# Selection state in PSUM, separate regions and locks, a loop of its own for the end, and earlier constants and loads, in a Fourier layer with routed experts

## The chip, the cores and the metric

The kernel runs on one core of a Trainium2 chip. Its engines are TensorE (PE; PEld is its weight load), VectorE (DVE), ScalarE (ACT), GpSimd (POOL) and SyncE (SP); transfers are issued on the queues of SP, ACT and POOL and carried by 16 DMA engines. The metric is the device time of one execution in microseconds, as the median of several runs; less is better.

## The reference

For each of 8 images x (3136 positions, 256 channels, float32) a Fourier layer is followed by a layer that sends 128 positions through a two-layer expert:

```python
X = rfft(x, axis=1)                              # 1569 frequencies
Yr = shrink(Xr @ w_r - Xi @ w_i + b_r, 0.01)     # shrink: sign(v) * max(|v| - 0.01, 0)
Yi = shrink(Xr @ w_i + Xi @ w_r + b_i, 0.01)
y = irfft(Yr + 1j * Yi)
scores = y @ w_gate                              # one per position
top = the 128 positions with the largest scores
out = y;  out[top] = y[top] + sigmoid(scores[top]) * (relu(y[top] @ w1) @ w2)
```

with w_r, w_i 256x256, w1 256x1024, w2 1024x256.

## The kernel before, in words

The transform of 3136 = 98 x 32 points is done in two stages of matmuls each way. Loads of x (`ld_x`) bring parts of an image, `fold` (on POOL in the steady state, 1.29 us for each of two instructions, line 392) adds and subtracts its halves, `s1` (line 403) does the first stage on PE and writes to a scratch array As in DRAM. The middle runs over 100 units, one per step t: `s2` (line 433) the second stage, read back from As; `spectral` (lines 226 to 228 and 466) the products with the weights, where ACT copies one part to SBUF (line 460), POOL adds the bias (line 462) and DVE adds both (line 466); `shrink` (lines 471, 473); and `s2i` (line 490) the first inverse stage, whose two PSUM tiles `pca` and `pcb` ACT copies to be stored to a scratch array Cs in DRAM (line 513) and DVE multiplies with the gate for the scores (line 501). `ld_c` loads Cs, `s1i` (line 550) does the last stage, and its results go to the output. An image has 8 pieces of `s1`, 12 or 13 units, and 8 pieces of `s1i`.

PE's banks of PSUM are full: pca and pcb are one bank each of 512 float32 per partition. Columns 0 to 255 hold the outputs of `s2i`. The second half of pcb holds a product of `spectral`; the second half of pca is shared by the routing: 64 columns for the counts of the selection (`sel_ps`), the rest for everything else (`route_ps`).

Routing is a set of Python generators, called threads, that are advanced once or twice per step by `turn` in phases "pe", "da", "db". A thread first computes scores (`score`, lines 518 to 527), then `select` finds the 128th largest score of each of its images by bits: per round DVE makes candidate words f from the threshold word w (line 243), compares all scores with them (line 247), sums (line 251); PE adds the counts over partitions (line 254); DVE turns the count into the next w (lines 266 to 269). A round takes one step: 17 rounds at 2 bits, 12 at 3 bits. Then `place` works out the indices (lines 276 to 327), four to five steps per image. The threads are images (0, 1) and (2, 3) at 2 bits, (4, 5), (6) and (7) at 3 bits. One lock, `lock`, is held by a thread while it scores or places an image, as both use route_ps. The experts are two more threads that `tick` advances once per step: `fetch` gathers the rows of an image, whose output must be complete, with an indirect transfer on POOL's queue; `ffn` (lines 340 to 374) takes ten turns per image, three of them idle, and uses one bank named "m".

The order of instructions on every engine and queue is that of the program. In step t the loop issues on SP the stores of the step before, loads of x for 21 steps later, loads of As 3 to 4 steps ahead, loads of Cs 2 steps ahead of use; then `s2` of the next unit, a piece of `s1` or `s1i`, the routing's phases, `spectral` with the phase "db" inside, the folds, the experts, `s2i` of the unit before, `shrink`. The loop runs on for 20 steps after the last unit with what is left: three pieces of image 6, all of image 7, whose Cs is loaded in steps 101 and 103, and routing. Constants of the routing are loaded and made in step 8 (`consts_b`, lines 211 to 217), and zeros for the padding rows of Cs in steps 8, 10 and 12 (`pads`, line 531, on POOL).

Of the kernel before, what the change touches and what calls it, by code (L numbers as in the profile page):

```python
# [10 lines left out]
F32 = mybir.dt.float32  # L11
# [89 lines left out]
def fourier_moe(ctx: ExitStack, tc: tile.TileContext, x, w_r, w_i, b_r, b_i, wg, w1, w2,  # L101
# [63 lines left out]

    sel_ps, route_ps = pca[:, D:D + 64], pca[:, D + 64:]

# [42 lines left out]
    def consts_b():  # L210
        ld(wq, t_wq)
        make_identity(nc, ident)
        ld(digits, t_dig)
        nc.gpsimd.dma_start(out=tm, in_=t_m)
        nc.gpsimd.iota(iota, [[1, 128 * NCHK]], base=0, channel_multiplier=0, allow_small_or_imprecise_dtypes=True)
        nc.gpsimd.iota(nrow, [[1, 1]], base=0, channel_multiplier=N2, allow_small_or_imprecise_dtypes=True)
        nc.gpsimd.iota(tcol, [[128, NCHK]], base=0, channel_multiplier=1, allow_small_or_imprecise_dtypes=True)

    def consts_moe(k):
# [10 lines left out]
    def select(bs, bits, thrs, at):  # L230
# [3 lines left out]
        while cuts[-1] > 0:  # L234
            cuts.append(max(cuts[-1] - bits, 0))
        w = None
        for hi, i in zip([32] + cuts, cuts):
            m = 2 ** (hi - i) - 1
            f = pool.tile([N1, nb, m], U32, name=f"f{nb}{m}", bufs=1)
            if w is None:  # L240
                nc.vector.memset(f, 0)
            else:
                nc.vector.tensor_tensor(out=f, in0=digits[:, 8 * i:8 * i + m].rearrange("p (o m) -> p o m", o=1).broadcast_to([N1, nb, m]),  # L243
                                        in1=w.broadcast_to([N1, nb, m]), op=ALU.bitwise_xor)
# [11 lines left out]
            tot = tot.rearrange("p (b m) -> p b m", b=nb)  # L256
            w2 = pool.tile([N1, nb, 1], U32, name=f"w{nb}")
            if w is None:
                nc.vector.tensor_scalar(out=w2.bitcast(I32), in0=tot, scalar1=cap - 0.5, scalar2=1.0, op0=ALU.is_ge, op1=ALU.subtract)
            else:  # L260
                d = pool.tile([N1, nb, 1], U32, name=f"d{nb}", bufs=1)
                if m == 1:
                    nc.vector.tensor_scalar(out=d, in0=tot, scalar1=cap - 0.5, scalar2=None, op0=ALU.is_ge)
                else:
                    ok = pool.tile([N1, nb, m], F32, name=f"ok{nb}{m}", bufs=1)
                    nc.vector.tensor_scalar(out=ok, in0=tot, scalar1=cap - 0.5, scalar2=None, op0=ALU.is_ge)  # L266
                    with nc.allow_low_precision(reason="whole numbers"):
                        nc.vector.tensor_reduce(out=d, in_=ok, axis=AX.X, op=ALU.add)
                nc.vector.scalar_tensor_tensor(out=w2, in0=d, scalar=i, in1=w, op0=ALU.logical_shift_left, op1=ALU.bitwise_xor)  # L269
            w = w2  # L270
        thr = pool.tile([N1, nb, 1], F32, name=f"thr{bs[0]}", bufs=1)
# [4 lines left out]
    def place(b, thr, slots):  # L276
# [4 lines left out]
        yield "pe"  # L281
        pt = route_ps[:2 * N2, :N1]
        nc.tensor.matmul(pt, mf, eye, start=True, stop=True)
# [3 lines left out]
        yield "pe"  # L287
        pp = route_ps[:N1, :2 * N2].rearrange("p (a c) -> p a c", a=2)
        nc.tensor.matmul(route_ps[:N1, :2 * N2], mt, upper[:2 * N2, :], start=True, stop=True)
        yield "da"  # L290
# [6 lines left out]
        yield "pe"  # L297
        pb = route_ps[:N1, :2]
        nc.tensor.matmul(pb, lower, cnt, start=True, stop=False)
# [5 lines left out]
        for k in range(NCHK):  # L305
# [8 lines left out]
            yield "pe"  # L314
            pi = route_ps[:n, :N2 + 2]
            for a in range(2):
# [12 lines left out]
    def gather(b, k, idx):  # L329
# [4 lines left out]
        return xe  # L334

    def prepare(b, k, idx, xe):
        n = min(128, cap - 128 * k)
# [13 lines left out]
    def hidden(b, k, xT, hs):  # L351
        n = min(128, cap - 128 * k)
        for q in range(FF // 512):
            ph = ps.tile([128, 4, n], F32, name="m", bufs=1)
            for f in range(4):
# [9 lines left out]
    def combine(b, k, idx, xe, ga, hs):  # L365
        n = min(128, cap - 128 * k)
        py = ps.tile([n, D], F32, name="m", bufs=1)
        for f in range(FF // 128):
# [147 lines left out]
    def score(b):  # L516
        p = route_ps[:NJ, :128]
# [5 lines left out]
        p = route_ps[:N1, :N2]  # L523
        for q in range(4):
            nc.tensor.matmul(p, wq[:, q, :], t[:, 64 * (q // 2) + q % 2:64 * (q // 2) + 64:2], start=(q == 0), stop=(q == 3))
        yield "da"
        nc.vector.tensor_copy(scores[:, b, :], p)

    def pads(k):
        z = pool.tile([128, 2, 2, 2 * D], F32, name="ot", bufs=2).rearrange("p r s x -> p (r s x)")  # L530
        nc.gpsimd.memset(z, 0.0)
        for q in range(2):
            ld(Csd[k][q, NH:].rearrange("m n d -> (m n d)").rearrange("(p x) -> p x", p=120), z[:120, :1024])

# [27 lines left out]
    def warm():  # L562
# [5 lines left out]
        for i in range(14):  # L568
            nc.tensor.matmul(p[:, i % 2], pr[:, :128], pr[:, :512], start=True, stop=True)

    YB, XB, KB, RB, AB = 2, 2, 1, 1, 3
    G, U = 13, 8
# [6 lines left out]

    lock = []  # L580

    def route(k, bs, bits):
        for b in bs:
            while done["s2i"] < b or lock:
                yield "pe"
            lock.append(k)
            yield from score(b)
            lock.clear()
            yield "da"
        yield from select(bs, bits, thrs, 32 * (k % 2))  # L590
        for b in bs:
            yield "db"
            while lock:
                yield "db"
            lock.append(k)
            yield from place(b, thrs[b], slots)
            lock.clear()

# [10 lines left out]
    def ffn():  # L609
        for e in range(B * NCHK):  # L610
            while not fetched:
                yield
            for _ in range(3):
                yield
            item = fetched[0]
            xT, ga = prepare(*item)
            yield
# [4 lines left out]

    threads = [[route(k, *a), "pe"] for k, a in enumerate((((0, 1), 2), ((2, 3), 2), ((4, 5), 3), ((6,), 3), ((7,), 3)))]
    ffns = [fetch(), ffn()]
# [30 lines left out]
    consts_a()  # L655
    consts_g(0)
    for i in range(U):
        fold(0, i, nc.gpsimd if i % 3 == 2 else nc.vector)
        s1(0, i)
        if i == 4:  # L660
            ld_x(1, 0)
            ld_x(1, 2)
        flush()
        issue_late()
# [8 lines left out]
    rest = [(b, i) for b in range(B) for i in range(U)]  # L673
    for t in range(-1, T + 20):
        flush()
# [4 lines left out]
        for u in (t + 3, t + 4):  # L680
            if 1 < u < T and (units[u][1] == G - 1) == (u == t + 3):
                ld_a(*units[u])
        for b, i in due(t - LAG + 2):
            if b < B - 1:
                ld_c(b, i)
        if t in (T + 1, T + 3):
            for i in range(4):
                ld_c(B - 1, i + 2 * (t - T - 1))
        if t % 2 == 0 and (t + 4) // 2 in range(2, 7):
# [45 lines left out]
        pair()  # L735
    flush()
    issue_late()
    while threads or ffns:
        turn("pe", "da", "db")
        tick(ffns)  # L740

# [26 lines left out]
```

## Time and profile before

| | us |
|---|---|
| median of 3 runs | 811.73 (802.27 to 816.13) |
| the profiled execution | 805.65 |
| its span, first to last instruction | 803.9 |

| engine | busy us | share of the span |
|---|---|---|
| PE | 657.2 | 82% |
| PEld | 490.1 | 61% |
| DVE | 515.5 | 64% |
| ACT | 361.6 | 45% |
| POOL | 299.7 | 37% |

The mean granted clock of TensorE is 0.919. The DMA engines moved 182.46 MB. Busy shares are means over the start, the 100 steps (to 717 us) and the end, which have different limits; the rows further down are therefore taken by stretch. In a row of a timeline, what stands in brackets is the engine's idle time before the instruction and what ended it. A wait that is put down to an instruction on DVE or ACT ended when that instruction did, in order of its queue.

### The profile page before, as it was taken

The numbers are of one execution on the slowest core, as the hardware profiler recorded it, in microseconds if no ns is written. First come the engines' busy times: TensorE is split into PE (matmuls) and PEld (weight loads), VectorE is DVE, ScalarE is ACT, GpSimd is POOL, SyncE is SP. The second block draws the span as 40 slices with busy tenths as digits, with TensorE's granted clock in tenths as the row PEclk, the third lists the DMA queues.
The fourth block names the chain that finished last, engine by engine and source line by source line (L and its number), as shares of the span: only waits on it lengthen the run. The fifth ranks groups of instructions, "written<-read, shape, count | busy, mean of one in ns | idle before, by whom it ended". The sixth has DMA issues, their size and how long they took to land. (4 is left out here: it accounts for less than half of the span.)

```text
span 803.9 us, 20190 instructions
## 1 busy us (share of the span) xinstructions
PE 657.2 (82%) x8148; PEld 490.1 (61%) x8148; DVE 515.5 (64%) x1327; ACT 361.6 (45%) x655; POOL 299.7 (37%) x247
## 2 busy tenths in 40 slices
PE   2649879997698788879899889989999787968765
PEld 0347667665476656556677667666677676734554
DVE  3526446653369887767647887786766989873550
ACT  1326445654354554445555553555644444433100
POOL 2227765543244434335434334335522221210001
PEclk9869979998899999989999999999999999986769
DMA  9988989998779885879997978869966655479400
GB/s 166 246 262 244 294 248 312 320 294 281 225 247 274 254 241 181 244 203 300 275 275 239 297 190 262 242 155 335 307 202 179 211 158 160 126 190 313 99 7 20
DMA packets 83988, 182.46 MB, mean 227 GB/s; under 512 B 7435, under 2 KB 60904, under 8 KB 75704
## 3 DMA queue, kind: packets, MB, share of 16 engines
q1 hardware_dynamic: 75544, 153.75, 61.9%
q10 hardware_dynamic: 7456, 25.27, 13.1%
q0 software_dynamic: 896, 2.17, 0.8%
q8 instruction: 64, 1.05, 0.6%
q14 instruction: 28, 0.23, 0.1%
HBM read 92.29 MB, written 88.93 MB: 225 GB/s over the span
## 5 line engine op out<-in xcount | busy, mean ns | idle before, releaser
L462 POOL TENSOR_TENSOR kb<-ks,bias 128x512 f32<-128x512 f32 x100 | 128.6, 1286 | 375.0 <-ACT ks L460 369.5
L392 POOL TENSOR_TENSOR sd<-xt 113x512 f32<-113x512 f32 x114 | 144.2, 1286 | 26.8 <-DMA xt<-in_x 26.8
L466 DVE TENSOR_TENSOR py<-py,kb 128x512 f32<-128x512 f32 x100 | 69.6, 696 | 106.6 <-POOL kb L462 77.3
L499 ACT COPY ct<-pcb 128x256 f32<-128x256 f32 (+1 forms) x100 | 37.1, 371 | 212.8 <-PE pcb L490 195.5
L446 DVE TENSOR_TENSOR Xl<-px,Xh 128x768 fp32r<-128x768 f32 x100 | 95.7, 957 | 36.0 <-ACT Xh L445 36.0
L490 PE MATMUL pca<-Y,gi_sb 64*64 64x256 f32 x768 | 105.6, 394 | 2.0 <-DVE ok L266 1.0
L490 PE MATMUL pcb<-Y,gi_sb 64*64 64x256 f32 x768 | 105.6, 394 | 0.0
L433 PEld LDWEIGHTS px<-g_sb,av 64*64 64x64 f32 x3072 | 78.5, 135 | 30.8 <-issue 18.5
L433 PE MATMUL px<-g_sb,av 64*64 64x96 f32 x3072 | 83.7, 246 | 10.3 <-DMA av<-As 8.4
L403 PE MATMUL s<-sd,w 49*64 49x512 f32 x480 | 67.0, 604 | 29.3 <-DVE sd L392 14.7
L471 ACT ACTIVATE r<-py,m2l 128x512 f32<-128x512 f32 x100 | 69.8, 698 | 45.6 <-DVE py L466 40.0
L445 ACT CAST Xh<-px 128x768 fp32r<-128x768 f32 x100 | 80.9, 809 | 18.5 <-PE px L433 18.5
L550 PE MATMUL s<-cv,wi_sb 49*64 49x512 f32 x464 | 64.7, 627 | 24.5 <-DMA cv<-Cs 18.6
L226 PE MATMUL pcb<-wsh,Xh 128*128 128x256 f32 x200 | 68.8, 344 | 8.0 <-DVE Csc L501 8.0
L552 ACT COPY ot<-s 128x1024 f32<-128x1024 f32 x58 | 59.6, 1028 | 25.1 <-PE s L550 25.1
L405 ACT COPY at<-s 128x1024 f32<-128x1024 f32 x58 | 60.0, 1034 | 23.2 <-PE s L403 23.2
L226 PEld LDWEIGHTS pcb<-wsh,Xh 128*128 128x128 f32 x200 | 40.0, 200 | 48.9 <-issue 23.8
L473 DVE SCALAR_TENSOR_TENSOR Y<-py,r 128x512 f32<-128x512 f32 x100 | 68.6, 686 | 0.8 <-ACT r L471 0.8
L501 DVE CUSTOM_DVE_ANT_0 junk<-pcb,wgb 128x256 f32<-128x256 f32 (+1 forms) x100 | 42.2, 422 | 41.2 <-ACT ct L499 38.4
L490 PEld LDWEIGHTS pca<-Y,gi_sb 64*64 64x64 f32 x768 | 46.2, 134 | 29.6 <-issue 3.5
L226 PE MATMUL py<-wnh,Xh 128*128 128x256 f32 x200 | 61.0, 305 | 0.9 <-DVE Y L473 0.9
L228 PE MATMUL py<-wnl,Xh 128*128 128x256 f32 x200 | 60.2, 301 | 0.0
(132 smaller groups left out, 1433.2 us busy)
## 6 DMA issues: line engine op xcount, KB each, us to landing
As<-at SPq DMA_DIRECT2D x30, 1024.0 KB
cv<-Cs SPq DMA_DIRECT2D x30, 1024.0 KB
av<-As SPq DMA_DIRECT2D x96, 256.0 KB
Cs<-ct SPq DMA_DIRECT2D x96, 256.0 KB
xt<-in_x ACTq DMA_DIRECT2D x30, 384.0 KB
xt<-in_x SPq DMA_DIRECT2D x30, 384.0 KB
out<-ot SPq DMA_DIRECT2D x30, 384.0 KB
out<-ot ACTq DMA_DIRECT2D x30, 384.0 KB
```

The costliest lines, as they stand in the source:

```text
L226: nc.tensor.matmul(out, wh, mh, start=start, stop=False)
L392: eng.tensor_tensor(out=f[:113, k], in0=t[:113, 0], in1=t[:113, 1], op=op)
L403: nc.tensor.matmul(p[64 * c:64 * c + 64, r, :], w[64 * r:64 * r + NH, c, :], f[64 * r:64 * r + NH, c], start=True, stop=True)
L433: nc.tensor.matmul(o[:, :, N2 * j:N2 * j + N2], a[64 * p:64 * p + 64, j, g % 2, 128 * h + 64 * q:128 * h + 64 * q + 64], g_sb[64 * p:64 * ...
L445: nc.scalar.copy(out=vh, in_=v)
L446: nc.vector.tensor_tensor(out=vl, in0=v, in1=vh.bitcast(F32), op=ALU.subtract)
L462: nc.gpsimd.tensor_tensor(out=kb[:r], in0=ks[:r].broadcast_to([r, 2, D]), in1=bias[:r], op=ALU.add)
L466: nc.vector.tensor_tensor(out=py[:r], in0=py[:r], in1=kb[:r], op=ALU.add)
L471: nc.scalar.activation(out=r1[:r], in_=py[:r], func=AF.Relu, bias=m2l[:r], scale=1.0)
L473: nc.vector.scalar_tensor_tensor(out=y[:r], in0=py[:r], scalar=0.0, in1=r1[:r], op0=ALU.min, op1=ALU.add)
L490: nc.tensor.matmul(p[q][64 * a:64 * a + 64], gi_sb[64 * q:64 * q + 64, g, c, 64 * a:64 * a + 64], y[64 * q:64 * q + 64, c, :], start=(c == ...
L550: nc.tensor.matmul(p[64 * c:64 * c + 64, r, :], wi_sb[64 * r:64 * r + NH], f[64 * r:64 * r + NH, 4 * c + 2 * e:4 * c + 2 * e + 2, :], star ...
```

## The change

- `select` keeps the threshold words w and the candidates f in PSUM, in 30 columns of pca beside the counts, instead of SBUF. Two threads can select at a time, by the parity of their number.
- The rest of pca's second half is cut into a region for places (98 columns) and one for scores (128 columns), each with its own lock; the two selection regions have locks too.
- The threads of images 4 and 5 are separate.
- `consts_b` keeps two loads at step 8; `make_identity`, the three iotas and the transfer of tm go into `consts_c`, which is issued before the first fold. The zeros for `pads` are filled once, by DVE, with 1024 elements instead of 2048.
- Loads of Cs are issued 3 steps ahead of use instead of 2.
- The steps after the last unit are a loop of their own: the last `s2i` first, then routing, then a piece of `s1i` (none in the fourth step, so image 7 comes in steps T+4 to T+11), then products of the weights with themselves into the bank "py" whose results nobody reads (`idle`), one after a piece, four without; then ACT's late stores and the experts. While threads are left after it, three such products per turn.
- The expert of image 7 uses three banks instead of one, and twelve such products are issued ahead of it.

```diff
-    sel_ps, route_ps = pca[:, D:D + 64], pca[:, D + 64:]
+    sel_ps, place_ps, score_ps = [pca[:, a:b] for a, b in ((D, D + 30), (D + 30, D + 128), (D + 128, 2 * D))]
...
     def consts_b():
         ld(wq, t_wq)
+        ld(digits, t_dig)
+
+    def consts_c():
         make_identity(nc, ident)
-        ld(digits, t_dig)
-        nc.gpsimd.dma_start(out=tm, in_=t_m)
         nc.gpsimd.iota(iota, [[1, 128 * NCHK]], base=0, channel_multiplier=0, allow_small_or_imprecise_dtypes=True)
         nc.gpsimd.iota(nrow, [[1, 1]], base=0, channel_multiplier=N2, allow_small_or_imprecise_dtypes=True)
         nc.gpsimd.iota(tcol, [[128, NCHK]], base=0, channel_multiplier=1, allow_small_or_imprecise_dtypes=True)
+        nc.gpsimd.dma_start(out=tm, in_=t_m)
...
-        w = None
+        words = [sel_ps[:N1, at + a:at + a + n * nb].bitcast(U32) for a, n in ((7, 2 ** bits - 1), (15 - nb, 1))]
+        w = words[1].rearrange("p (b m) -> p b m", b=nb)
         for hi, i in zip([32] + cuts, cuts):
             m = 2 ** (hi - i) - 1
-            f = pool.tile([N1, nb, m], U32, name=f"f{nb}{m}", bufs=1)
-            if w is None:
+            f = words[0][:, :nb * m].rearrange("p (b m) -> p b m", b=nb)
+            if hi == 32:
                 nc.vector.memset(f, 0)
...
-                nc.vector.scalar_tensor_tensor(out=w2, in0=d, scalar=i, in1=w, op0=ALU.logical_shift_left, op1=ALU.bitwise_xor)
-            w = w2
+                nc.vector.scalar_tensor_tensor(out=w, in0=d, scalar=i, in1=w, op0=ALU.logical_shift_left, op1=ALU.bitwise_xor)
...
+    def bank(b, name):
+        return name if b == B - 1 else "m"
...
-            ph = ps.tile([128, 4, n], F32, name="m", bufs=1)
+            ph = ps.tile([128, 4, n], F32, name=bank(b, ("s", "m")[q % 2]), bufs=1)
...
-        py = ps.tile([n, D], F32, name="m", bufs=1)
+        py = ps.tile([n, D], F32, name=bank(b, "px"), bufs=1)
...
+    zero = []
+
     def pads(k):
-        z = pool.tile([128, 2, 2, 2 * D], F32, name="ot", bufs=2).rearrange("p r s x -> p (r s x)")
-        nc.gpsimd.memset(z, 0.0)
+        if not zero:
+            zero.append(pool.tile([128, 2, 2, 2 * D], F32, name="ot", bufs=2)[:, 0].rearrange("p s x -> p (s x)"))
+            nc.vector.memset(zero[0], 0.0)
...
+    def idle(n):
+        p = ps.tile([128, 2 * D], F32, name="py", bufs=1)
+        for i in range(n):
+            nc.tensor.matmul(p, wts[0][0][:, 0, :128], wts[0][0].rearrange("p h d -> p (h d)"), start=True, stop=True)
...
-    lock = []
+    locks = set()
+
+    def hold(key, phase):
+        while key in locks:
+            yield phase
+        locks.add(key)
 
     def route(k, bs, bits):
         for b in bs:
-            while done["s2i"] < b or lock:
+            while done["s2i"] < b:
                 yield "pe"
-            lock.append(k)
+            yield from hold("score", "pe")
             yield from score(b)
-            lock.clear()
+            locks.discard("score")
             yield "da"
-        yield from select(bs, bits, thrs, 32 * (k % 2))
+        yield from hold(k % 2, "da")
+        yield from select(bs, bits, thrs, 15 * (k % 2))
+        locks.discard(k % 2)
         for b in bs:
             yield "db"
-            while lock:
-                yield "db"
-            lock.append(k)
+            yield from hold("place", "db")
             yield from place(b, thrs[b], slots)
-            lock.clear()
+            locks.discard("place")
...
             item = fetched[0]
+            if item[0] == B - 1:
+                idle(12)
...
-    threads = [... (((0, 1), 2), ((2, 3), 2), ((4, 5), 3), ((6,), 3), ((7,), 3)))]
+    threads = [... (((0, 1), 2), ((2, 3), 2), ((4,), 3), ((5,), 3), ((6,), 3), ((7,), 3)))]
...
     consts_a()
     consts_g(0)
+    consts_c()
...
-    for t in range(-1, T + 20):
+    for t in range(-1, T):
...
-        for b, i in due(t - LAG + 2):
+        for b, i in due(t - LAG + 3):
             if b < B - 1:
                 ld_c(b, i)
-        if t in (T + 1, T + 3):
-            for i in range(4):
-                ld_c(B - 1, i + 2 * (t - T - 1))
...
-    flush()
-    issue_late()
+    for t in range(T, T + 20):
+        flush()
+        for b, i in due(t - LAG + 3):
+            if b < B - 1:
+                ld_c(b, i)
+        if t in (T + 1, T + 3):
+            for i in range(4):
+                ld_c(B - 1, i + 2 * (t - T - 1))
+        if t == T:
+            s2i(*units[T - 1])
+            done["s2i"] = B - 1
+        turn("pe", "da", "db")
+        if rest and t != T + 3:
+            b, i = rest.pop(0)
+            s1i(b, i)
+            if i == U - 1:
+                done["s1i"] = b
+            idle(1)
+        else:
+            idle(4)
+        issue_late()
+        tick(ffns)
     while threads or ffns:
+        flush()
         turn("pe", "da", "db")
+        if threads:
+            idle(3)
         tick(ffns)
```

## Rows read from the trace of the kernel before

**Rows 1.** Page, 40 slices of 20.1 us: clock, DMA share, rate.

```profile
PEclk9869979998899999989999999999999999986769
DMA  9988989998779885879997978869966655479400
GB/s 166 246 262 244 294 248 312 320 294 281 225 247 274 254 241 181 244 203 300 275 275 239 297 190 262 242 155 335 307 202 179 211 158 160 126 190 313 99 7 20
```

**Rows 2.** Windows of line 466: length, DVE busy (count), clock, DMA share, GB/s.

```profile
130.00:185.00 55.00, 7.00 (x10) 1.00 0.94 285
242.00:357.60 115.60, 11.09 (x16) 0.91 0.80 238
441.70:537.60 95.90, 8.99 (x14) 0.93 0.78 229
610.70:717.00 106.30, 11.05 (x16) 0.98 0.57 171
```

**Rows 3.** Groups by form: count, busy us, mean ns, idle before, releasers.

```profile
L269 DVE SCALAR_TENSOR_TENSOR w<-d,w 98x2 uint32<-98x2 uint32 x43 | 34.9, 811 | 1.5
...
L247 DVE TENSOR_TENSOR c<-scores,f 98x192 bf16<-98x192 f32 x30 | 24.3, 809 | 0.9
...
L243 DVE TENSOR_TENSOR f<-digits,w 98x6 uint32<-98x6 uint32 x30 | 16.3, 544 | 1.0
...
L247 DVE TENSOR_TENSOR c<-scores,f 98x224 bf16<-98x224 f32 x20 | 7.8, 389 | 0.4
...
L569 PE MATMUL px<-Xh 128*128 128x512 f32 x14 | 5.7, 586 | 5.1 <-ACT Xh L566 5.1
```

**Rows 4.** Timeline near 641 us, POOL and DVE: start, length, instruction.

```profile
641.37 1.27 POOL L462 TENSOR_TENSOR kb<-ks,bias 128x512 f32<-128x512 f32 x1 [4.93 <-ACT ks L460]
...
641.56 1.11 DVE L269 SCALAR_TENSOR_TENSOR w<-d,w 98x2 uint32<-98x2 uint32 x1
...
647.63 0.16 DVE L269 SCALAR_TENSOR_TENSOR w<-d,w 98x2 uint32<-98x2 uint32 x1
```

**Rows 5.** Waits of PE: who, for whom, us in total, times, longest.

```profile
PE pca L254 <- DVE Csc L501: 33.7, 20, 3.0
...
PE s L550 <- DMA cv<-Cs: 18.6, 7, 5.6
...
PE pca L254 <- DVE n L251: 7.8, 5, 2.1
```

**Rows 6.** Timeline near 643 us, DVE and PE.

```profile
642.79 0.27 DVE L521 COPY sct<-pca 25x128 f32<-25x128 f32 x1
...
643.12 0.43 PE L490 MATMUL pca<-Y,gi_sb 64*64 64x256 f32 x2 [0.85 <-DVE sct L521]
```

**Rows 7.** Timeline of POOL and DVE, at the start and at the constants.

```profile
17.86 2.96 POOL L392 TENSOR_TENSOR sd<-xt 113x512 f32<-113x512 f32 x2 [13.57 <-DMA xt<-in_x]
...
91.44 0.70 DVE L466 TENSOR_TENSOR py<-py,kb 128x512 f32<-128x512 f32 x1 [1.59 <-POOL kb L462]
...
101.74 0.76 POOL L214 DMA_DIRECT2D tm<-t_m  x1 [3.12 <-issue]
...
104.19 0.70 DVE L466 TENSOR_TENSOR py<-py,kb 128x512 f32<-128x512 f32 x1 [9.44 <-POOL kb L462]
```

**Rows 8.** Timeline of SP and PE at a load of Cs.

```profile
184.27 0.33 SPq L153 DMA_DIRECT2D cv<-Cs  x1
...
191.73 1.98 PE L550 MATMUL s<-cv,wi_sb 49*64 49x512 f32 x8 [5.14 <-DMA cv<-Cs]
```

**Rows 9.** Timeline of PE: an expert's piece in the loop, and the end.

```profile
655.00 1.05 PE L357 MATMUL m<-xT,w1s 128*128 128x128 f32 x8
...
745.72 0.29 PE L518 MATMUL pca<-ident,Csc 128*25 128x128 f32 x1
...
774.16 2.08 PE L357 MATMUL m<-xT,w1s 128*128 128x128 f32 x8
```

**Rows 10.** Windows, all engines: busy us (count), clock, DMA share, GB/s.

```profile
0.00:223.60 223.60, 169.89 (x2144) 121.55 (x2144) 103.64 (x219) 97.66 (x174) 107.07 (x92) 0.89 0.90 262
```

More of the change, by code (lines that the diff above doesn't have):

```diff
@@ L256, in select @@
             tot = tot.rearrange("p (b m) -> p b m", b=nb)
-            w2 = pool.tile([N1, nb, 1], U32, name=f"w{nb}")
-            if w is None:
-                nc.vector.tensor_scalar(out=w2.bitcast(I32), in0=tot, scalar1=cap - 0.5, scalar2=1.0, op0=ALU.is_ge, op1=ALU.subtract)
+            if hi == 32:
+                nc.vector.tensor_scalar(out=w.bitcast(I32), in0=tot, scalar1=cap - 0.5, scalar2=1.0, op0=ALU.is_ge, op1=ALU.subtract)
             else:
@@ L281, in place @@
         yield "pe"
-        pt = route_ps[:2 * N2, :N1]
+        pt = place_ps[:2 * N2, :N1]
         nc.tensor.matmul(pt, mf, eye, start=True, stop=True)
@@ L287, in place @@
         yield "pe"
-        pp = route_ps[:N1, :2 * N2].rearrange("p (a c) -> p a c", a=2)
-        nc.tensor.matmul(route_ps[:N1, :2 * N2], mt, upper[:2 * N2, :], start=True, stop=True)
+        pp = place_ps[:N1, :2 * N2].rearrange("p (a c) -> p a c", a=2)
+        nc.tensor.matmul(place_ps[:N1, :2 * N2], mt, upper[:2 * N2, :], start=True, stop=True)
         yield "da"
@@ L297, in place @@
         yield "pe"
-        pb = route_ps[:N1, :2]
+        pb = place_ps[:N1, :2]
         nc.tensor.matmul(pb, lower, cnt, start=True, stop=False)
@@ L314, in place @@
             yield "pe"
-            pi = route_ps[:n, :N2 + 2]
+            pi = place_ps[:n, :N2 + 2]
             for a in range(2):
@@ L516, in score @@
     def score(b):
-        p = route_ps[:NJ, :128]
+        p = score_ps[:NJ, :128]
         nc.tensor.transpose(out=p, in_=Csc[b], identity=ident)
@@ L522, in score @@
         yield "pe"
-        p = route_ps[:N1, :N2]
+        p = score_ps[:N1, :N2]
         for q in range(4):
@@ L527, in score @@
         nc.vector.tensor_copy(scores[:, b, :], p)
+    zero = []
     def pads(k):
-        z = pool.tile([128, 2, 2, 2 * D], F32, name="ot", bufs=2).rearrange("p r s x -> p (r s x)")
-        nc.gpsimd.memset(z, 0.0)
+        if not zero:
+            zero.append(pool.tile([128, 2, 2, 2 * D], F32, name="ot", bufs=2)[:, 0].rearrange("p s x -> p (s x)"))
+            nc.vector.memset(zero[0], 0.0)
         for q in range(2):
-            ld(Csd[k][q, NH:].rearrange("m n d -> (m n d)").rearrange("(p x) -> p x", p=120), z[:120, :1024])
+            ld(Csd[k][q, NH:].rearrange("m n d -> (m n d)").rearrange("(p x) -> p x", p=120), zero[0][:120])
     def ld_c(b, i):
@@ L621, in ffn @@
             fetched.pop(0)
-    threads = [[route(k, *a), "pe"] for k, a in enumerate((((0, 1), 2), ((2, 3), 2), ((4, 5), 3), ((6,), 3), ((7,), 3)))]
+    threads = [[route(k, *a), "pe"] for k, a in enumerate((((0, 1), 2), ((2, 3), 2), ((4,), 3), ((5,), 3), ((6,), 3), ((7,), 3)))]
     ffns = [fetch(), ffn()]
```

## Prediction

> **What bounds the kernel now.** I read the page's slices first [rows 1]. TensorE (PE) is nearly always busy until 700 us, and the DMA engines are close to full until about 600 us; so neither alone explains the stretches in which PE drops to six or seven tenths. Then I counted steps: the add of line 466 runs once per step, so its count in a window gives the length of a step [rows 2]. Without a selection a step takes 55.0/10 = 5.5 us. With one it takes 115.6/16 = 7.2 us, 95.9/14 = 6.9 us and 106.3/16 = 6.6 us. The selection adds little arithmetic, so I asked which of its instructions are too long [rows 3]. On 98x2 words line 269 takes 811 ns; line 243 takes 544 ns on 98x6; line 247 takes 809 ns on 192 elements and 389 ns on 224. A timeline shows why [rows 4]: VectorE (DVE) starts line 269 at 641.56, while GpSimd (POOL) runs its add of line 462 from 641.37 for 1.27 us, and is done just after it; the next one, with POOL idle, takes 0.16 us. Held are DVE instructions whose two tensors both lie in SBUF, behind a POOL instruction that reads SBUF. PE pays in the list of waits [rows 5]: the counting matmul of line 254 waited 33.7 us behind line 501, the DVE work of the step before, which the held instructions had made late. The same list has 18.6 us on loads of Cs. Two more places stand out: line 466 waits 9.44 us for POOL near 100 us [rows 7], and the end after 711 us, where the clock digits fall to 6 and 7 [rows 1] and the last selection starts only at 745.72 [rows 9].
>
> **The change part by part**, against the profiled execution's 805.65 us (span 803.9; the median of the runs shown is 811.73, 6 us above).
>
> *POOL's constants first, pads on DVE.* Line 466 runs at 91.44 and next at 104.19 [rows 7], 12.8 us apart where a step without a selection takes 5.5: 7.3 us late, behind line 531's fill, the identity and the 3.12 us without work before line 214 on POOL's queue. The lower clock behind it (a 7 as the sixth digit [rows 1]) stretches the next steps by an estimated 2 us. Moved before the loop, the constants lie where POOL waits 13.57 us for x [rows 7]: free. The fill, half as wide and once instead of three times, falls on DVE, which waits in that step: free. The DMA engines were at 8 to 9 tenths all through this stretch, so a little of it comes back as lateness: **8 us**, bounds 2 and 9.3.
>
> *Cs loaded a step earlier.* Line 550 waits 5.14 us at 191.73 for a load that SP issued only at 184.27 [rows 8], 7.5 us before; it is one of seven waits, of which the longest is 5.6 us [rows 5]. A step is 5.5 to 7 us, so the lead covers each of them if SP reaches the load a step earlier. On SP's queue it passes one step's stores and loads of x and As, which then start up to one issue later; they have leads of their own. Its buffer was last read more than a step before. SP waits in order, and may stand just as long elsewhere, so I take half, **9 us**, bounds 0 and 18.6.
>
> *Threshold words and candidates in PSUM.* Lines 243, 247 and 269 then have one tensor in SBUF. Held time: line 269 43 x (811-160) = 28 us, line 247 30 x (809-389) = 13 us, line 243 30 x (544-160) = 12 us, 53 us in all. On the path is what PE lost, line 254's 33.7 us, and the half clock that follows such a gap: windows at 0.91, 0.93 and 0.98 [rows 2] are 10.4 + 6.7 + 2.1 = 19 us of lost clock, of which I take half, 9 us. Against it stands a new wait. The matmul of line 490 writes the bank in which the candidates now lie, so it must wait until line 247 has read them. That this binds across the two halves of a bank is in the trace: line 490 waited 0.85 us for line 521, which reads the other half [rows 6]. Line 247 ends some 2.7 us after the step's line 501 (lines 473 and 446, four instructions of 0.16, itself 0.39), the products of the weights some 2.3 us after it; 0.4 us of waiting, nothing where a piece of the experts (1.05 us [rows 9]) stands between, as in six steps of ten. There are 66 rounds in the loop: 26 x 0.4 = 10 us. Images 4 and 5, now single, start 12 steps earlier and overlap the pair (2, 3) and each other for some 8 steps, which cost the full 0.85 us: 7 us. So 33.7 + 9 - 16 = **27 us**, bounds 0 and 53. DVE's form of line 247 with 448 elements disappears. Operations on PSUM are taken to be no longer: line 466, which reads and writes PSUM, takes 0.70 us for 512 elements [rows 7], in proportion less than line 247's 389 ns for 224. Own locks and regions for scores and places cost nothing; they let a score pass while a place is under way.
>
> *The end.* Before, image 7's scores wait for the lock until 745.72 [rows 9], and its twelve rounds, places and expert follow one another to the end. After, they begin at once, and twelve rounds and four steps of places lie beside the last inverse stage and the experts. The experts are one thread of ten turns per image, and the one of image 3 ends shortly before the loop does, as before, so images 4 to 7 stay in the end; only their first turn comes 3 turns earlier. PE's time there: full clock gives back up to 1.03 us per piece (2.08 at 774.16 against 1.05 at 655.00 [rows 9]), about nine pieces and some inverse pieces, 10 us; the waits on the counts 7.8 us [rows 5], of which all lie in the end; 2 us as the last matmuls of line 490 are issued ahead of a step's other work; 1.5 us from separate banks for the last expert; 3 us for the turns. That is 24 us. Fillers: 11 x 1 + 9 x 4 + 12 = 59 products of 128x512, at most 0.41 us each (14 took 5.7 us in the warm-up [rows 3]), half that at full clock; those that stand beside a DVE round are covered, and I charge 8 us. **16 us**, bounds 0 and 24.
>
> Sum: 8 + 9 + 27 + 16 = 60 us, 805.65 - 60 = 746; since the median stood a little above this execution, I say **748 us**.
>
> **The rivals.**
>
> *The transfers bind (chance 0.18).* 0.90 of the DMA engines' time is used in the first 223.6 us [rows 10]. At the best slice, 335 GB/s [rows 1], the bytes of that stretch (262 x 223.6) need 175 us, and in the windows of selections the share is 0.78 to 0.80 [rows 2], so that a step of 7.2 us can't fall under 5.8. For it: loads already come late. Against: steps of 5.5 us run at a share of 0.94 [rows 2]. Then constants and Cs give 2 us each and the selection 14, the end its 16: 805.65 - 34 = 772. The Trainium skill (SBUF — State Buffer, Summary: rules for kernel authors) puts transfers between HBM and SBUF at about 358 GB/s. By that figure the first stretch would need an estimated 164 us and this rival would be weaker; no slice here reaches it.
>
> *The end does not shorten (0.12).* Fillers and the experts' chain fill PE, and the half clock stays: the end gives 2 instead of 16, 760 us.
>
> *Slower, by the bank (0.03).* POOL's add still gates line 466, so freeing DVE gains nothing, and each of the 66 rounds puts line 490 behind line 247, 0.85 us alone and about 2 us in the 8 double ones: 58 x 0.85 + 8 x 2 = 65 us. With constants 2, Cs 0 and the end 16 on the other side: 805.65 + 47 = 853. It decides where line 247 ends later than the experts' piece and the products by more than the held time it saved. Against it: only one long wait of that kind stands in the trace. The Trainium skill (PSUM — Partial Sum Buffer, PSUM bank collisions raise a hardware error) says to guard PSUM by bank and group of 32 partitions, not by address; by that rule every one of these rounds is a candidate for the wait, as rows 6 show for one.
>
> *The change does not free DVE (in the 0.05 for no change).* If a PSUM operand still left line 243 or 247 held, selection would give nothing and the extra rounds cost some: 805.65 - 33 + 16 = 789, near the border.
>
> **Numbers.** Forecast 0.62, transfers 0.18, end 0.12, bank 0.03, not freed 0.05. The forecast's own range is 728 to 766 (about a third of the terms either way); eight in ten with the first two rivals is 722 to 782. A measurement of this kernel can tell about 2% from no change. Faster by more (below 795): all of forecast, transfers and end and most of the last, 0.93; within 2% 0.04; slower 0.03.
>
> **What would show it.** Lines 269 and 243 at 0.16 to 0.17 us and line 247 at 0.39 throughout; line 254's wait under 10 us; a new wait of line 490 on line 247 of 10 to 20 us; line 466 no longer waiting near 100 us; waits on Cs under 8 us; selection steps near 6 us; the last score near 715 us and a clock near full to the end. I am wrong if steps stay near 7 us with DMA at 0.95, or if PE's idle time only moves to line 490.

## The result, and the profile after

The changed kernel takes **768.56 us** (median of 4 runs, 762.78 to 771.12) against 813.18 before: a ratio of 0.9514, 95% interval 0.938 to 0.9647. It is faster, and inside the predicted range of 722 to 782, but 20 us slower than the 748 I gave. Run again beside the last experiments it took 767.56, a ratio of 0.9494 [0.9448, 0.954]. The profiled execution took 769.65 us, with a span of 767.7.

The page's clock slices of the changed kernel (tenths of full speed) answer to [rows 1]:

```profile
PEclk9869999999899999899999999999999999997799
```

The clock digits between slices 8 and 36 are now nearly all 9; two 7s are left behind the loop.

Windows of the add of the products (line 470, before 466), with its count, clock, DMA share and rate, answer to [rows 2]:

```profile
226.10:333.80 107.70, 11.84 (x17) 0.97 0.87 270
412.90:506.30 93.40, 9.73 (x14) 0.98 0.88 268
506.30:587.60 81.30, 7.62 (x11) 0.98 0.75 228
587.60:682.50 94.90, 11.15 (x16) 1.00 0.62 178
```

A step with a selection now takes 6.3, 6.7, 7.4 and 5.9 us. The third window is the one to look at: its 11 steps are the slowest of the loop, although the DMA share there is lower than in the two before.

Groups by form of the selection's DVE work (count, busy us, mean ns) answer to [rows 3]:

```profile
L250 DVE TENSOR_TENSOR c<-scores,pca 98x224 bf16<-98x224 f32 x40 | 15.3, 383 | 0.9
L250 DVE TENSOR_TENSOR c<-scores,pca 98x192 bf16<-98x192 f32 x30 | 10.6, 352 | 0.9
L313 DVE SCALAR_TENSOR_TENSOR hot<-iota,end,hot 98x128 f32<-98x128 f32 x16 | 10.4, 651 | 0.6
L312 DVE TENSOR_SCALAR hot<-iota,row 98x128 f32<-98x128 f32 x16 | 8.6, 536 | 0.0
...
L271 DVE SCALAR_TENSOR_TENSOR pca<-d,pca 98x2 uint32<-98x2 uint32 x32 | 5.3, 165 | 1.1
L246 DVE TENSOR_TENSOR pca<-digits,pca 98x6 uint32<-98x6 uint32 x30 | 5.1, 170 | 1.0
```

The shift (line 271) fell from 811 to 165 ns, the xor (246) from 544 to 170, the compare on 192 elements (250) from 809 to 352. Lines 312 and 313, which write the one-hot rows of the places into SBUF, are still held.

PE's waits answer to [rows 5]:

```profile
PE pca L494 <- DVE c L250: 15.3, 19, 3.4
PE px L437 <- DMA av<-As: 15.2, 6, 7.3
PE pca L257 <- DVE Csc L505: 14.8, 12, 5.0
...
PE px L445 <- DMA av<-As: 6.1, 3, 3.0
...
PE s L557 <- DMA cv<-Cs: 1.4, 1, 1.4
```

The counting matmul's wait (257) has halved. A new wait of line 494 for the compare stands beside it. The wait for Cs is nearly gone (1.4 us, from 18.6), but the waits for As rose from 8.4 us to 15.2 + 6.1.

For all kernels below I read where the steps begin: the start of the add of the products in one profiled execution each, in us, counted from step 0; "behind" is from the start of step 99 to the end of the span.

| kernel | step 10 | step 11 | step 45 | step 72 | step 83 | step 99 | behind |
|---|---|---|---|---|---|---|---|
| before | 115.8 | 120.7 | 347.7 | 537.6 | 605.2 | 711.4 | 92.5 |
| changed | 107.5 | 119.8 | 329.2 | 506.4 | 587.7 | 682.6 | 85.1 |
| changed, run again | 107.0 | 120.3 | 327.5 | 504.6 | 586.0 | 680.8 | 85.2 |
| words alone | 114.7 | 119.6 | 326.5 | 502.3 | 568.8 | 670.6 | 96.8 |
| words back in SBUF | 107.7 | 119.2 | 335.4 | 528.3 | 610.9 | 708.8 | 87.1 |
| constants late | 113.7 | 118.6 | 323.2 | 502.7 | 585.4 | 680.2 | 83.1 |
| Cs two steps ahead | 109.0 | 121.8 | 336.8 | 509.8 | 591.2 | 686.7 | 88.1 |
| pair (4, 5) | 107.3 | 119.7 | 328.0 | 502.4 | 572.5 | 670.6 | 86.5 |
| compare first | 106.7 | 117.6 | 324.2 | 498.3 | 579.9 | 674.6 | 85.1 |
| other bank first | 106.5 | 119.0 | 328.6 | 504.0 | 584.3 | 677.4 | 85.1 |
| no fillers | 109.0 | 122.6 | 328.2 | 504.8 | 587.6 | 682.4 | 75.4 |

The two rows of the changed kernel show how far one execution's steps repeat: within 2 us. The changed kernel led by 8.3 us at step 10 and by 0.9 at step 11; by 31.2 at step 72 and by only 17.5 at step 83. In these two places it lost what it had won. A few executions ran longer than the others at a lower clock: the ratios leave them out, three of the four of the pair without fillers and the profiled one of the four edits among them, but the ratio of the words alone still holds two, 783.94 and 783.6 us.

### The profile page after: what moved, and what is told of

It is laid out like the page before. It is cut to its first block, busy times and chain, and to the rows that moved or that the text cites. A ratio compares the mean times of both kernels' runs of the same rounds, so it can differ in the third digit from the quotient of the medians.

```text
span 767.7 us, 20397 instructions
## 1 busy us (share of the span) xinstructions
PE 660.9 (86%) x8219; PEld 485.1 (63%) x8219; DVE 476.4 (62%) x1398; ACT 360.7 (47%) x655; POOL 293.3 (38%) x244
## 4 chain that ended last, share of the span: by engine, by line
PE 48%; DMA 21%; DVE 15%; ACT 6%; issue 6%; POOL 2%; SPq 2%; POOLq 0%; DVEq 0%; ACTq 0%
PE pca L494 8%; DMA xt<-in_x 8%; DMA av<-As 6%; PE s L407 5%; PE px L437 4%; PE py L228 4%; PE py L229 3%; PE py L230 3%; DVE junk L505 3%; PE s L557 3%; PE pcb L228 3%; PE m L361 3%; DMA As<-at 3%; PE m L373 2%; DVE Xl L450 2%
## 5 line engine op out<-in xcount | busy, mean ns | idle before, releaser
L494 PE MATMUL pca<-Y,gi_sb 64*64 64x256 f32 x768 | 105.5, 394 | 17.8 <-DVE c L250 15.3
L437 PEld LDWEIGHTS px<-g_sb,av 64*64 64x64 f32 x3072 | 80.1, 137 | 40.6 <-issue 17.3
L437 PE MATMUL px<-g_sb,av 64*64 64x96 f32 x3072 | 86.6, 250 | 18.3 <-DMA av<-As 15.2
L407 PE MATMUL s<-sd,w 49*64 49x512 f32 x480 | 75.1, 657 | 25.4 <-DVE sd L396 14.2
L449 ACT CAST Xh<-px 128x768 fp32r<-128x768 f32 x100 | 81.3, 813 | 32.6 <-PE px L437 25.7
L228 PE MATMUL pcb<-wsh,Xh 128*128 128x256 f32 x200 | 66.9, 335 | 1.1 <-DVE Csc L505 1.1
L228 PE MATMUL py<-wnh,Xh 128*128 128x256 f32 x200 | 58.4, 292 | 1.1 <-DVE Y L477 1.1
L230 PE MATMUL pcb<-wsl,Xh 128*128 128x256 f32 x200 | 57.5, 288 | 0.0
```

Source lines behind the costliest of these rows:

```text
L228: nc.tensor.matmul(out, wh, mh, start=start, stop=False)
L230: return nc.tensor.matmul(out, wh, ml, start=False, stop=stop).ins
L407: nc.tensor.matmul(p[64 * c:64 * c + 64, r, :], w[64 * r:64 * r + NH, c, :], f[64 * r:64 * r + NH, c], start=True, stop=True)
L437: nc.tensor.matmul(o[:, :, N2 * j:N2 * j + N2], a[64 * p:64 * p + 64, j, g % 2, 128 * h + 64 * q:128 * h + 64 * q + 64], g_sb[64 * p:64 * ...
L449: nc.scalar.copy(out=vh, in_=v)
L494: nc.tensor.matmul(p[q][64 * a:64 * a + 64], gi_sb[64 * q:64 * q + 64, g, c, 64 * a:64 * a + 64], y[64 * q:64 * q + 64, c, :], start=(c == ...
```

## The experiments

My theory at this point was that the words had given some 18 us, that the early constants had been given back on loads of As, that the lead of Cs had paid, and that the new wait of line 494 was behind the loss after step 72. The main rival was that the transfers bind and the words hardly count.

**Words alone**, in the kernel before:

```diff
-        w = None
+        words = [sel_ps[:N1, at + a:at + a + n].bitcast(U32) for a, n in ((14, 14), (30, 2))]
+        w = words[1][:, :nb].rearrange("p (b m) -> p b m", b=nb)
...
-            f = pool.tile([N1, nb, m], U32, name=f"f{nb}{m}", bufs=1)
+            f = words[0][:, :nb * m].rearrange("p (b m) -> p b m", b=nb)
```

> The kernel before with one edit: the threshold word and the candidates of the selection lie in the selection's region of the PSUM bank; nothing else of the change. My theory: what the change gained in the selection's steps came from these words alone, about 18 us, and the bank's new wait took part of it back. So some 793 to 798 us against 813 before; the held durations fall to 0.17 us (xor, shift) and 0.39 us (compare), and a wait of the inverse's first matmul on the compare of 10 to 20 us appears. Rival 1 (transfers bind, the words are hidden): 808 to 815 us although the durations fall. Rival 2 (the gain comes from all other parts together with the words): under 5 us here.

Measured: 779.24 us against 810.23, ratio 0.9642 [0.9597, 0.9687]. This one edit is worth 29 us by the ratio, 31 by the medians, and 36 if the two longest of its five runs are left out (median 774.69). That is clearly more than I had allowed it: my 18 was wrong. Its waits (columns as above) are these:

```profile
PE pca L489 <- DVE c L248: 11.6, 24, 2.2
...
PE pca L255 <- DVE Csc L500: 4.9, 6, 0.9
```

The wait of the counting matmul behind the step's DVE work fell from 33.7 us [rows 5] to 4.9, with the bank's new wait already there at 11.6. The table has the surprise: without any other part of the change this kernel begins step 99 at 670.6, 12 us ahead of the changed kernel, and takes 66.5 us from step 72 to 83 where the changed one takes 81.3 (before: 67.6). The profiled execution, 769.14 us, is the shortest of its five, so the 12 us may be a few too many. Something else in the change costs time in these steps.

**Words back in SBUF**, in the changed kernel:

```diff
-            f = words[0][:, :nb * m].rearrange("p (b m) -> p b m", b=nb)
+            f = pool.tile([N1, nb, m], U32, name=f"f{at}{m}", bufs=1)
...
+            w2 = pool.tile([N1, nb, 1], U32, name=f"w{at}{nb}")
```

> The changed kernel with the word and the candidates back in SBUF tiles, everything else of the change kept. My theory: it loses what the words gave, 18 to 25 us: 786 to 794 us against 769; the xor and shift are held again (0.5 to 1.1 us a piece), the wait of the inverse's first matmul on the compare stays near 15 us or grows, since the compare comes later. Rival 1 (transfers bind): at most 4 us slower, 773. Rival 2 (the bank's wait takes all that the words give): 765 to 770, and that wait under 4 us.

Measured: 801.43 us, ratio 0.9881 [0.9845, 0.9916]: 33 us slower than the changed kernel (31 by the ratios), against an expected 18 to 25. Both ends of the comparison agree on some 30 us. The held durations are back, for the same forms of the same program:

```profile
L271 DVE SCALAR_TENSOR_TENSOR w<-d,w 98x2 uint32<-98x2 uint32 x32 | 24.8, 775 | 1.1
L249 DVE TENSOR_TENSOR c<-scores,f 98x192 bf16<-98x192 f32 x30 | 23.2, 772 | 0.8
```

And so is the wait:

```profile
PE pca L256 <- DVE Csc L506: 32.3, 21, 3.0
```

The new wait of line 494 for the compare does not stand in the list of this kernel's larger waits, so I missed there: it needs the candidates in PSUM. Yet steps 72 to 83 take 82.6 us, as slow as in the changed kernel. The loss there needs neither the words in PSUM nor the bank's wait.

**Constants late**, in the changed kernel:

```diff
-    consts_c()
     for i in range(U):
...
         if t == 8:
             consts_b()
+            consts_c()
```

> The changed kernel with identity, iotas and the table of places made in step 8 again, as before the change (on POOL, behind the pads' fill that stays on VectorE). My theory: the early constants gave a lead of 8 us at step 10 that was lost again to late loads of As in steps 10 and 11, so the time stays within 3 us of the changed kernel: 766 to 772. Step 8 is some 5 us longer, and the waits on As in steps 10 and 11 shorter. Rival (the lead is kept, and later steps lose for other reasons): 8 us slower, 776 to 778.

Measured: 767.36 us, ratio 0.9484 [0.9429, 0.9538]: as the changed kernel. The early constants are worth nothing that can be seen. PE's waits from 96 to 122 us, first in the changed kernel:

```profile
PE px L445 <- DMA av<-As: 4.7, 2, 3.0
```

then with the constants late:

```profile
PE pcb L228 <- DVE Csc L505: 5.8, 1, 5.8
```

One wait stands in for the other. Windows of line 470 over the same steps of the changed kernel show with what:

```profile
97.90:107.50 9.60, 1.40 (x2) 1.00 0.94 334
107.50:125.30 17.80, 1.40 (x3) 0.81 1.01 320
```

From step 8 to step 10 two steps take 9.6 us, at the pace of the steps before them, while the transfers' share is 0.94, then 1.01; the next two take 17.8 us, with the waits for As and a clock of 0.81 behind them (the third add counted there is the one at the window's end). The chain that ended last shows what these steps stand on (changed kernel; start, length):

```profile
99.53 6.73 DMA As<-at
106.32 6.76 DMA av<-As
```

The matmul that waits, line 445, reads As of images 0 and 1, whose last piece was stored only at 99.53, and the load follows that store's landing. So the lead is lost on a store and a load one after the other, while the transfers are full. Whether their order or the rate set the 13.5 us was not tested.

**Cs two steps ahead**, in the changed kernel, both loops:

```diff
-        for b, i in due(t - LAG + 3):
+        for b, i in due(t - LAG + 2):
```

> The changed kernel with Cs loaded two steps ahead again, in both loops. My theory: the wait of the last inverse stage on its load comes back, from 1.4 us to some 15 to 24 us, of which half shows: 774 to 782 us. Rival 1 (SP stands as long elsewhere, so a step's lead only moves the wait): 766 to 771, and the waits on As fall by what those on Cs rise. Rival 2 (the lead is worth its full wait): 786 or more.

Measured: 778.88 us, ratio 0.9611 [0.9546, 0.9676]: 8 to 10 us slower, by ratio or by time, as expected. Its waits:

```profile
PE s L557 <- DMA cv<-Cs: 20.5, 7, 7.6
...
PE px L437 <- DMA av<-As: 5.8, 1, 5.8
...
PE px L445 <- DMA av<-As: 3.5, 1, 3.5
```

The waits on Cs rise by 19 us, those on As fall by 12 (from 21.3 to 9.3). So the longer lead moves more than half of the wait from one load to another, and what is left pays.

**Pair (4, 5)**. The change had also given images 4 and 5 a selection each (three bits a round) where before they shared one. Here they share one again, with two bits, since three do not fit the smaller region:

```diff
-    threads = [... ((4,), 3), ((5,), 3), ((6,), 3), ((7,), 3)))]
+    threads = [... ((4, 5), 2), ((6,), 3), ((7,), 3)))]
```

> The changed kernel with one selection for images 4 and 5 together again (two bits a round, as for the first two pairs) in place of one for each; words in PSUM, own regions, own loop and lead kept. Behind it stands that the words alone made the kernel before 31 us faster, with the loop's last step 12 us earlier than in the changed kernel, which lost 14 us in steps 72 to 83. My theory: there image 4's rounds run beside the places of images 2 and 3, and the masks and one-hot rows of the places, held by POOL, stand ahead of image 4's compare on VectorE, which the inverse's first matmul awaits. With the pair, steps 72 to 83 take some 6 us again and the time falls by 10 to 15 us: 754 to 759 against 769. Rival 1 (the places do it by themselves): 766 to 771, the loss stays. Rival 2 (the end gets longer as image 5 is chosen later): the loop 14 us shorter, the tail longer by as much, 766 to 771.

Measured: 759.39 us, ratio 0.9367 [0.9301, 0.9432], against 0.9494 [0.9448, 0.954] for the changed kernel: 8 to 12 us faster, by time or by ratio, and the time lies just past the slow end of what my theory gave. Steps 72 to 83 take 70.1 us. Windows over 12 adds each (PE, PEld, DVE, ACT and POOL busy with counts, clock, DMA share, rate), first the changed kernel, then this one:

```profile
506.00:588.00 82.00, 69.23 (x927) 52.01 (x928) 64.00 (x194) 39.61 (x72) 28.56 (x24) 0.98 0.75 227
```

```profile
502.00:573.00 71.00, 66.45 (x914) 50.38 (x907) 49.79 (x142) 39.37 (x72) 28.98 (x24) 1.00 0.88 271
```

PE, ACT and POOL do nearly the same work in both. DVE does 14 us less in the second, and the stretch is 11 us shorter. What DVE does more in the changed kernel is read from its groups in that window, first the changed kernel's:

```profile
L312 DVE TENSOR_SCALAR hot<-iota,row 98x128 f32<-98x128 f32 x6 | 5.3, 878 | 0.0
L313 DVE SCALAR_TENSOR_TENSOR hot<-iota,end,hot 98x128 f32<-98x128 f32 x6 | 4.9, 822 | 0.2
...
L250 DVE TENSOR_TENSOR c<-scores,pca 98x224 bf16<-98x224 f32 (+1 forms) x12 | 4.2, 347 | 0.2
```

then with the pair:

```profile
L313 DVE SCALAR_TENSOR_TENSOR hot<-iota,end,hot 98x128 f32<-98x128 f32 x4 | 2.5, 620 | 0.1
L250 DVE TENSOR_TENSOR c<-scores,pca 98x192 bf16<-98x192 f32 (+1 forms) x6 | 2.0, 332 | 0.2
...
L312 DVE TENSOR_SCALAR hot<-iota,row 98x128 f32<-98x128 f32 x4 | 1.1, 280 | 0.0
```

In the changed kernel image 4's rounds run until 552.77, beside the places of images 2 and 3 (one-hot rows from 511.93 and 542.85), and image 5's from 559.14, beside the places of image 4. With the pair the places of images 2 and 3 (506.95 and 531.54) are done before its selection starts at 545.64: no round stands beside them. Of the 14 us, 6.6 are one-hot rows: twelve instructions instead of eight, and seven of them held, where the pair has one (line 312 takes 878 ns on average, with the pair 280). The rest is mostly twelve rounds in place of six.

**Compare first**, in the changed kernel: the places' masks and one-hot rows in a phase of their own ("dc"), issued on DVE behind the compares of the same step.

```diff
-            yield "db"
+            yield "dc"
...
-            py, r = spectral(*units[t], lambda: turn("db"))
+            py, r = spectral(*units[t], lambda: turn("db", "dc"))
```

> The changed kernel with the places' masks and one-hot rows issued on VectorE behind the compares of the same step, not ahead of them by the order of the images. Theory: the waits of the inverse's first matmul on the compare of 2 to 3.4 us in steps 72 to 80 go, 8 to 12 us in all: 757 to 761. Rival: the held work only moves, to ahead of the add of the products and the reduction behind it, and the time stays within 4 us of 769.

Measured: 765.8 us, ratio 0.9463 [0.9399, 0.9526], not to be told from the changed kernel's. The longest of the waits in question is in the changed kernel's timeline (POOL, DVE and PE; start, length, idle time before in brackets):

```profile
512.20 1.28 POOL L466 TENSOR_TENSOR kb<-ks,bias 128x512 f32<-128x512 f32 x1 [6.02 <-ACT ks L464]
512.24 1.38 DVE L313 SCALAR_TENSOR_TENSOR hot<-iota,end,hot 98x128 f32<-98x128 f32 x1
...
516.46 0.43 PE L494 MATMUL pca<-Y,gi_sb 64*64 64x256 f32 x2 [3.37 <-DVE c L250]
```

With the compare ahead of them that wait goes, but another comes; PE's waits in steps 72 to 83 of this kernel:

```profile
PE pca L318 <- DVE Csc L505: 5.9, 2, 3.5
...
PE pca L494 <- DVE c L250: 0.5, 2, 0.4
```

In the changed kernel the last of these is 10.1 us in the same steps, and line 318's 0.4. The steps still take 81.6 us (579.9 - 498.3), at a clock of 0.92 where the changed kernel had 0.98. So my theory fell and the rival held: DVE's work only moved. On the chain that ended last, DVE's pieces in these steps add up to 27 us in the changed kernel and 27 here, but to 9 with the pair: what DVE does there, the held rows included, sets these steps, and not its order. Which part of it, the rounds or the places of image 4, no run separates.

**Other bank first**, in the changed kernel:

```diff
-            for c in range(2):
-                for q in range(2):
+            for q in (1, 0):
+                for c in range(2):
```

> The changed kernel with the inverse's eight matmuls in another order: the four that write the other bank first, the four that write the bank of the candidates after them. A matmul takes 0.38 us and two run beside each other, so the first that must wait for the compare comes some 0.8 us later. Theory: the wait of that matmul on the compare falls from 15.3 us to under 7, and the time by 4 to 8 us: 761 to 765. Rival: the wait turns up at the counting matmul behind it or at the next product, and the time stays within 3 us of 769.

Measured: 765.46 us, ratio 0.9457 [0.938, 0.9534]. The wait of line 494 fell as expected, from 15.3 us in 19 cases to

```profile
PE pca L494 <- DVE c L250: 6.6, 4, 2.4
```

but whether the time followed can't be told: the interval holds the changed kernel's 0.9494. Step 99 comes 3 to 5 us earlier in the one execution shown.

**No fillers**, in the changed kernel: all 59 filler products of the end removed.

```diff
-            if item[0] == B - 1:
-                idle(12)
...
-            idle(1)
-        else:
-            idle(4)
...
-        if threads:
-            idle(3)
```

> The changed kernel without any of the filler products of the end: none in the end's turns and not the twelve ahead of the last expert. Theory: most stand where PE would wait, the twelve cost 3.1 us on the path, and the clock in the end falls somewhat more often: 763 to 771. Rival 1 (they hold the clock, and that is what shortened the end): 776 to 785, with more stretches at half clock behind the loop. Rival 2 (all of them cost their own time, some 15 us): 752 to 756.

Measured: 760.33 us, ratio 0.9433 [0.9342, 0.9524]. The interval overlaps the changed kernel's, but the traces, one execution each, are plain: step 99 begins at the same time, and what follows takes 75.4 us instead of 85.1. Windows of PE from step 99 on (busy with count, clock, DMA share, rate), the changed kernel and this one:

```profile
682.60:768.00 85.40, 71.67 (x406) 0.87 0.44 132
```

```profile
682.40:758.00 75.60, 57.58 (x348) 0.84 0.47 149
```

The fillers add 14 us of PE work, and the clock is 0.87 with them, 0.84 without. The time lies between two of my three cases, 763 to 771 and 752 to 756: the fillers cost two thirds of the 15 us I had put on their own time. That they shorten the end by holding the clock is refuted here: they hold it a little, and the end is longer. The twelve ahead of the last expert stand in the changed kernel's timeline between its matmuls and those of the expert before, from 751.76 for 3.12 us.

**Four edits together.** Pair (4, 5), no fillers, other bank first, and the experts' three idle turns counted from the gather on (this last part is shown, the others as above):

```diff
-            for _ in range(3):
+            while turns[0] - fetched[0][4] < 3:
                 yield
```

> The changed kernel with what the runs so far point to, together: one selection for images 4 and 5, no filler products, the inverse's matmuls of the other bank first, and the experts' three idle turns counted from the gather on, not from the end of the expert before. Theory: the pair gives 12 us and the fillers 8 to 10, as alone, the order of banks 2 to 4, the turns 3 to 6 in the end: 738 to 748 us. Rival (the gains share the same waits): 750 to 756, no better than the pair without fillers.

Measured: **745.13 us** (741.28 to 753.73), ratio 0.9207 [0.9156, 0.9257], against 767.56 for the changed kernel on the same chip: 22 us faster than it and 62 faster than before. This is the best of the kernels.

**Pair without fillers**, two of the four:

> The changed kernel with one selection for images 4 and 5 and without fillers, nothing else. Theory: the two gains lie in different places (steps 72 to 83, and behind the loop) and add up: 745 to 752 us. Rival (with the pair, image 5's places come later and the end waits for them, so the fillers stood beside a wait): 755 to 760.

Measured: 761.41 us (748.33 to 764.73), with no ratio. The runs lie too far apart to decide between the two: the shortest is in the theory's 745 to 752, the others are at 760.87 or more, past the rival's 755 to 760.

Whether the two gains add up stays open, and so does what the order of the banks and the turns add by themselves in the kernel of four edits.

**The four edits, Cs two steps ahead**:

> The kernel with all four edits (pair of images 4 and 5, no fillers, other bank first, turns from the gather on), and the loads of Cs two steps ahead as before the change. Theory: the third step of lead takes some 19 us of waits on Cs away and puts 12 on As in their place, so this one is 5 to 9 us slower than the one with three steps. Rival (with the pair kept, the loop ended at 670.6 with the lead as without it, so the lead is worth nothing): within 3 us of it.

Measured: 762.51 us, ratio 0.9437 [0.937, 0.9505]: 17 us slower than with three steps, where I expected 5 to 9. The waits on Cs are 24.8 us here, those on As 10.6 against 23.8 with three steps (profiled executions of 756.82 and 753.73 us). The lead looks worth more where the rest is faster, 17 us against 10, but by the intervals each of these is known to some 7 us only, so this is not shown. The **changed kernel again** ran beside these:

> The changed kernel itself, beside the three others on the same chip, as their yardstick. Theory and rivals expect the same: 765 to 771 us.

Measured: 767.56 us.

## Why the prediction was right in sign and 20 us too low

**What bounds the kernel.** Right: held DVE instructions made the counting matmul late, and freeing them is worth some 30 us, shown from both sides (29 to 36 with the words alone, 31 to 33 with the words taken back). The durations came out as read from the form of one held and one free instruction [rows 4]: 0.165, 0.170 and 0.383 us (0.352 for the smaller compare). The sum of the parts was 60 us; from the same 805.65 the changed kernel gained 37. Most of what is missing is in three terms: 8 us of the constants, some 9 of the end and 1 to 5 of the split.

**Words, 27 = 33.7 + 9 - 16.** The 16 holds 7 us for the split of images 4 and 5; without them the sum gives 33 us for the words alone, and 29 to 36 were measured. No run shows the 9 us of clock by itself. The new wait is where I put it and of its size: 15.3 us, predicted 10 to 20. On that wait the Trainium skill (PSUM — Partial Sum Buffer, PSUM bank collisions raise a hardware error) was a sound guide: guarding by bank, not by address, puts a wait into rounds whose regions are apart, and the trace agrees with 19 of them. The counting matmul's wait fell below 10 us, as said, with the words alone (4.9), but not in the whole change (14.8).

**The split of images 4 and 5.** This is the first step that failed. I saw the overlap, priced it as 8 steps at the full wait of 0.85 us, 7 us inside the 16, and looked for it at the bank. A wait of that size did come: line 494 waits 15.3 us for the compare, and 7.4 with the pair. But moving the compare ahead takes this wait away and leaves the steps as long as before. The split costs 8 to 12 us, and on DVE: the rounds and the held one-hot rows fill DVE to 64 of 82 us. I had counted what the edit removed (the form on 448 elements) and not that the rounds of two single selections would run beside the places, whose one-hot rows then fall beside POOL's adds.

**Constants, 8.** The second. The mechanism at POOL was right: line 470 comes at 97.93 and 102.68 without the gap of [rows 7]. But the value is 0, below my lower bound of 2. I had named "a little" of lateness from the DMA engines as what comes next; of the lead of 8.3 us 0.9 is left at step 11, on the store and load of As. This is near the rival of transfers that bind, which gave this term 2 us; but that rival spoke of the rate, and the chain shows a store and a load in series.

**Cs, 9.** Right, at 8 to 10, and for the reason named in the text: much of the wait comes back on the same queue, here 12 of 19 us as loads of As.

**The end, 16 = 24 - 8.** The third. Behind step 99 the time fell by 7.4 us (92.5 to 85.1). Without fillers it falls by 17.1. The charge for the fillers was right (9.7, predicted 8); the gain was 24 on paper and 17 measured. I expected the full clock to give back 10 us; the clock there is 0.87 (0.78 before), with two stretches at half, from 689 to 697 and from 713 to 721 us, one of them in this window of PE:

```profile
713.00:723.00 10.00, 10.00 (x44) 0.51 0.65 176
```

**Rivals.** By the number alone, 768.56 is next to the 772 of "the transfers bind". Its mechanism holds, if at all, for the constants only: Cs paid in full, and the selection gave far more than its 14. "The bank" (slower) and "not freed" are refuted by the words alone. "The end does not shorten" was half true. The forecast's own range of 728 to 766 was missed by 2.6 us; the wider one held because of the two rivals, though neither was what made the kernel slower as a whole. That is in part luck. As for the rate by which I weighed them: 335 GB/s is a mean over 20.1 us, and a window of 10 us of the same trace, in the end, held more:

```profile
724.00:734.00 10.00, 7.88 (x37) 0.50 1.01 400
```

So a best slice is a floor for what transfers can do for a moment, not their limit, and over a long stretch they do less: the best 20 us of the changed kernel have 360 GB/s, its best 40 us 324. By the 358 GB/s of the Trainium skill (SBUF — State Buffer, Summary: rules for kernel authors) this rival would have been weaker; the measurement lies above that figure over 10 us, at it over 20 and below it over 40.

## What to carry to other kernels

A gain at one stage is kept only if the next supplier can follow: follow the stores and loads right behind the stage, and where one waits for the other and the DMA share is already near 1, count the lead as lost until a run shows it kept. When work is split or regrouped, count the work that will run side by side on each engine per step, and compare that engine's busy time with the step, rather than pricing a single wait. Fillers that keep the clock up must be charged their whole length on the path until a run without them shows otherwise.

## What was not expected of the hardware

The one-hot rows, with SBUF operands only, take 0.28 us alone (line 312 at its shortest, 278 ns) and up to 1.35 us while POOL runs its adds; in the slow steps they average 0.88 us. The held time thus did not end with the words: it moved to the next instructions of that kind, which took 4.5 us in steps 72 to 83 before and take 10.2 now. PE at 9 tenths of busy time was granted half clock all the same, in the pair (4, 5), right behind a stretch with only 6.72 us busy of 10.4:

```profile
670.60:681.00 10.40, 6.72 (x48) 0.64 0.28 95
681.00:691.00 10.00, 9.49 (x41) 0.50 0.87 287
```
